# A linear-attention and maxout kernel: eight filling matmuls ahead of a unit's scores become four, between its two score blocks

## The chip, the cores and the metric

The kernel runs on one core of a Trainium2 chip. The metric is the device time in microseconds of one execution. Engines are named as in the profile: PE (TensorE, matmuls; PEld is its weight load), DVE (VectorE), ACT (ScalarE), POOL (GpSimd) and SP (SyncE, which issues most transfers).

## What is computed

Two parts follow each other. The first is a linear attention with a decaying state, for 4 batches, 8 heads, 768 steps and a head size of 48:

```python
for t in range(S):
    cur = np.einsum('bhd,bhe->bhde', u[None] * kt, vt)
    y[:, :, t] = np.einsum('bhd,bhde->bhe', rt, state + cur)
    state = wt[:, :, :, None] * state + np.einsum('bhd,bhe->bhde', kt, vt)
```

The second takes its output as 3072 tokens of 384 numbers through two projections to 1024, takes the larger of the two, and projects back to 384:

```python
h1 = x @ w1
h2 = x @ w2
g = np.maximum(h1, h2)
return (g @ w_out).astype(np.float32)
```

Inputs and output are float32. The kernel uses max(a, b) = relu(a - b) + b: it forms w1 - w2, and folds w2 with w_out into one matrix.

## The kernel before

**Units.** The work is cut into segments of 256 steps. A unit is one segment of one or two batches; there are eight. Units 0 to 3 are the first segment of one batch each, units 4 and 5 the second segment of two batches each, units 6 and 7 the third. Unit 0's work on heads is cut in two halves besides. Within a segment, two neighbouring steps lie on one partition (called j or i, 0 or 1), so 128 partitions hold 256 steps.

**Steps of a unit.** Loads of w, r, k and v; products and logarithms of w; prefix sums by a matmul with a triangle (`ex`, L398); exponentials; r and k scaled by the decays (`scale`, L176 or L180: the tiles rp and kp); their transposes on PE (`tr`, L565) and the copy of these out of PSUM to the tile RK (`te`, L168); the sum of k times v over the segment (`kv`, L596) and its addition to the state (`st`: a copy on ACT and T at L615); the scores of k against r (`sc`, L641); the masked copy of the scores into the tile M (`mk`, L650), whose diagonal has been set from products of r, k and u (`rk` and `ru` for the tile rku, `dg`, `dd`, `di` at L516) and whose other half is zeroed (`zero.M`, L257); the unit's outputs from M and v and from the state (`ya` L688, `yi` L675); then the second part (`gt` L706, `rl` L717, `op` L725 and L729) and its store.

**Scores of unit 0.** `sc.b.j.y` is one block: batch b of the unit, neighbour j, half y of the heads. For unit 0 a block has eight small matmuls. Both blocks of one half share one pair of PSUM banks; a masked copy `mk.b.j.y` takes one block out. The second half's blocks (y = 1) are issued some steps earlier; the blocks sc.0.0.1.0 and sc.0.0.0.0 are the first half's.

**Order.** Every step of every unit stands in one list written out by hand (ORDER, L53 to L114). A loop issues them in that order; each engine takes its own instructions in this order, and waits are set where a step needs another engine's result or a buffer. The letter behind @ names the engine (a for ACT, d for DVE, p for POOL).

**Buffers.** PSUM has four single banks (G), which fills, transposes, prefix sums and turned weights share, and two pairs (Y) for state sums, scores and outputs. A bank that comes free is given to the next step that asks.

**Fills.** `hot.n.x` issues n matmuls of 128x128 by 128x512 on S_b, whose results nobody reads:

```python
def hot(n, _):
    t = bank(F32, "G")
    zz = S_b[:, 0].rearrange("p b q e d -> p (b q e d)")
    for _ in range(n):
        nc.tensor.matmul(t, zz[:, 0:P], zz[:, 0:512], start=True, stop=True)
```

There are six rows of eight in the list, all in its first part (hot.8.0 to hot.8.5). On PE the order around the change is: second transposes of unit 1 (tr.1.0.1), hot.8.1, sc.0.0.1.0, sc.0.0.0.0, hot.8.4, the state sum of unit 1 (kv.1), its other transposes (tr.1.0.0).

## Time and profile before

| | |
|---|---|
| time, median of 3 runs | 146.99 us (146.61 to 147.71) |
| the profiled execution | 147.59 us |
| its span, first to last instruction | 145.9 us |
| busy: PE, DVE, ACT, POOL | 135.3, 116.0, 90.5, 89.3 us |
| fills (L234) | 47 records, 13.3 us busy, mean 435 ns |
| chain that ended last, by engine | PE 42%, DVE 36%, issue 7%, ACT 6% |

Times inside the span count from its start. In a timeline row stand the start, the time that the row took, engine, line, operation, output, inputs, shape and count; idle time ahead of the row and what ended it are in brackets. A row of several matmuls is as long as from the first's start to the last's end; they overlap. One matmul record in some dozens can be missing from a trace.

### The profile page before, as it was taken

The page shows a single profiled execution, that of the slowest core. Times are in us where ns is not written, and L with a number is a line of the kernel's source. Part 1 is how long each engine was busy: PE and PEld are TensorE (multiplying, and loading weights), DVE is VectorE, ACT ScalarE, POOL GpSimd, SP SyncE. Part 2 cuts the span into 40 slices and gives each one's busy share as a digit, 9 for nine tenths or more (in the row PEclk, how much of TensorE's full clock was granted, in tenths as well). Part 3 has the DMA queues.
Part 4 walks back from the last instruction along what each step waited for, and adds up shares of the span by engine and source line. Part 5 has one row for each costly group of instructions (what it writes and reads, how often), then busy time and mean ns, then how long its engine had stood idle before and what let it go on. Part 6 is the DMA issues. An engine that isn't in the chain of part 4 may idle for free.

```text
span 145.9 us, 5536 instructions
## 1 busy us (share of the span) xinstructions
PE 135.3 (93%) x2403; PEld 83.4 (57%) x2404; DVE 116.0 (80%) x162; ACT 90.5 (62%) x164; POOL 89.3 (61%) x106
## 2 busy tenths in 40 slices
PE   5999999789999999999997996999999999999990
PEld 2345654568756757875652563654557545664550
DVE  2489999999999999999998697799966689361411
ACT  4053794997999857999248499378358492227010
POOL 7659979996996389499792917803999900000000
PEclk9999999999999999999999999999999999999999
DMA  3999999999889999986989999699973980061014
GB/s 97 324 324 357 326 415 384 375 311 306 214 220 324 203 264 246 311 220 125 289 130 208 233 309 232 118 137 252 262 250 67 180 214 11 0 216 59 4 62 154
DMA packets 71187, 31.84 MB, mean 218 GB/s; under 512 B 66294, under 2 KB 70391, under 8 KB 71163
## 3 DMA queue, kind: packets, MB, share of 16 engines
q1 hardware_dynamic: 71162, 31.49, 82.9%
q8 instruction: 19, 0.31, 0.9%
q14 instruction: 6, 0.04, 0.1%
HBM read 23.61 MB, written 4.73 MB: 194 GB/s over the span
## 4 chain that ended last, share of the span: by engine, by line
PE 42%; DVE 36%; issue 7%; ACT 6%; POOL 3%; DMA 2%; SPq 2%; DVEq 0%; ACTq 0%
PE G L729 12%; DVE M L650 9%; PE G L706 9%; PE G L234 6%; PE G L725 5%; DVE rp L176 4%; DVE rku L176 3%; DVE dg L502 3%; DVE M L516 3%; DMA RK<-kp 2%; PE Y L688 2%; ACT gT L717 2%; PE Y L641 2%; POOL rku L180 2%; DVE kp L176 2%
## 5 line engine op out<-in xcount | busy, mean ns | idle before, releaser
L729 PE MATMUL G<-wo_sb,gT 128*128 128x384 bf16 x192 | 35.1, 326 | 0.0
L706 PE MATMUL G<-xT,wd_sb 128*128 128x256 bf16 (+1 forms) x192 | 34.2, 326 | 0.6 <-ACT xT L168 0.6
L650 DVE CAST_PREDICATED M<-mask,Y 128x1024 bf16<-128x1024 int32 (+1 forms) x26 | 28.6, 1133 | 4.4 <-PE Y L641 3.6
L717 ACT ACTIVATE gT<-G 128x512 bf16<-128x512 f32 x43 | 24.3, 600 | 10.7 <-PE G L706 10.4
L729 PEld LDWEIGHTS <-gT 128*128 128x128 bf16 x192 | 18.8, 98 | 12.4
L706 PEld LDWEIGHTS <-wd_sb 128*128 128x128 bf16 x192 | 17.9, 98 | 12.4 <-DVE wd_sb L176 0.6
L180 POOL TENSOR_TENSOR kp<-lk,iE 128x384 bf16<-128x384 f32 x16 | 17.1, 1099 | 8.5 <-DVE lk L176 4.2
L725 PE MATMUL G<-wc_sb,xT 128*128 128x384 bf16 x72 | 15.7, 327 | 0.0
L180 POOL TENSOR_TENSOR rku<-rku,u_b 128x384 f32<-128x384 f32 x14 | 14.4, 1052 | 2.0 <-DVE rku L176 2.0
L234 PE MATMUL G<-S_b 128*128 128x512 bf16 x47 | 13.3, 435 | 1.8 <-DVE S_b L263 1.8
L168 ACT COPY RK<-G 128x1024 bf16<-128x1024 bf16 x12 | 12.1, 1017 | 4.7 <-PE G L565 4.7
L168 ACT COPY osb<-G 128x384 f32<-128x384 f32 x7 | 3.3, 478 | 15.2 <-PE G L729 11.9
L180 POOL TENSOR_TENSOR rku<-lr,lk 128x384 f32<-128x384 f32 x8 | 10.5, 1341 | 3.6 <-issue 2.3
L641 PE MATMUL Y<-RK 48*64 48x128 bf16 x384 | 9.0, 220 | 2.6 <-DVE M L650 1.4
L502 DVE TENSOR_REDUCE dg<-rku 128x16 f32<-128x768 f32 x12 | 11.0, 944 | 0.1
L641 PEld LDWEIGHTS <-RK 48*64 48x64 bf16 x384 | 6.1, 106 | 7.8 <-issue 5.9
L168 ACT CAST xT<-Y 128x768 bf16<-128x768 f32 x7 | 7.0, 1027 | 5.7 <-PE Y L675 4.4
L234 PEld LDWEIGHTS <-S_b 128*128 128x128 bf16 x48 | 5.1, 111 | 8.1 <-issue 2.9
L516 DVE TENSOR_TENSOR M<-identq,gd 128x512 int32<-128x512 int32 x12 | 9.2, 778 | 0.4 <-POOL gd L168 0.3
L387 ACT ACTIVATE lg<-lg 128x768 f32<-128x768 f32 (+2 forms) x9 | 5.6, 628 | 6.0 <-DVE lg L176 5.4
L168 ACT CAST S_b<-S_f 64x768 bf16<-64x768 f32 (+1 forms) x14 | 8.7, 623 | 1.0 <-DVE S_f L612 0.8
L176 DVE TENSOR_TENSOR rp<-lr,G 128x768 bf16<-128x768 f32 (+2 forms) x11 | 8.8, 800 | 0.6 <-ACT G L436 0.6
(111 smaller groups left out, 237.5 us busy)
## 6 DMA issues: line engine op xcount, KB each, us to landing
lk<-in_k_dram SPq DMA_DIRECT2D x12, 384.0 KB, 4.9
lv<-in_v_dram SPq DMA_DIRECT2D x12, 384.0 KB, 5.5
lr<-in_r_dram SPq DMA_DIRECT2D x10, 384.0 KB, 5.2
lw<-in_w_dram SPq DMA_DIRECT2D x9, 384.0 KB, 5.1
out_dram<-osb SPq DMA_DIRECT2D x14, 192.0 KB, 4.3
gT<-in_moe_w_dram SPq DMA_DIRECT2D x4, 512.0 KB, 8.4
out_dram<-wb SPq DMA_DIRECT2D x10, 192.0 KB, 2.1
wso<-in_moe_w_out_dram SPq DMA_DIRECT2D x4, 384.0 KB, 5.3
```

The lines of the kernel that those rows point to most:

```text
L168: (nc.scalar.copy if e == "a" else nc.vector.tensor_copy if e == "d" else nc.gpsimd.tensor_copy)(o, i)
L176: op(o, a, b)
L180: op(o[:, g], a[:, g], b[:, g])
L234: nc.tensor.matmul(t, zz[:, 0:P], zz[:, 0:512], start=True, stop=True)
L502: nc.vector.reduce_sum(s.dg[:, b].rearrange("p i h -> p h i"), s.rku[:, b], axis=AX.X)
L516: (nc.vector if en == "d" else nc.gpsimd).tensor_tensor(out=o, in0=m, in1=g.unsqueeze(3).to_broadcast([P, 2, H, Q // 2]), op=ALU.bitwise_and)
L641: nc.tensor.matmul(t[q * Q:(q + 1) * Q, e, p * P:(p + 1) * P].rearrange("s (i g) -> s i g", i=2), s.kT[d, b, j, y * n + p, q, :], s.rT[d, ...
L650: nc.vector.copy_predicated(t[:, :, 2 * n * y:2 * n * (y + 1)].rearrange("s i (p e) g -> s p e i g", e=2), mask[:, j].bitcast(I32).unsquee ...
L706: nc.tensor.matmul(t[:, m * n * P:(m + 1) * n * P].rearrange("c (b t) -> c b t", t=P), wd_sb[:, ko, fo * P:(fo + 1) * P], s.xT[:, 0:n, ko, :],
L717: nc.scalar.activation(o, i, AF.Relu)
L725: nc.tensor.matmul(t[:, 0:HD], s.xT[:, a, ko, :], wc_sb[:, ko, :], start=(ko == 0), stop=False)
L729: nc.tensor.matmul(t[:, 0:HD], s.gT[:, c:c + P], wo_sb[:, f, :], start=False, stop=(f == FO - 1))
```

## The change

The row hot.8.1 is taken out of its place ahead of both blocks of unit 0's first half. A row of four of the same matmuls, hot.4.1, is put in between the two blocks, behind sc.0.0.1.0 and ahead of sc.0.0.0.0. So the program has 44 fills in place of 48. Between the old place and the new stand, for other engines, a load of weights (wload.1.1) and three products of unit 2 (ru.2.0, kw.2.0, scale.2.1.0.0), and for PE the first score block; nothing else changes its order.

```diff
-te.1.0.1@a rk.2.0@d zero.M.2@p di.0.0@d ie.2.0 zero.M.0@p rw.2.0@d hot.8.1 wload.1.1 ru.2.0@d
-kw.2.0@p scale.2.1.0.0@p sc.0.0.1.0 sc.0.0.0.0 mk.0.0.1.0 vb.1.0@a hot.8.4 mk.0.0.0.0 mk.0.0.1.1
+te.1.0.1@a rk.2.0@d zero.M.2@p di.0.0@d ie.2.0 zero.M.0@p rw.2.0@d wload.1.1 ru.2.0@d kw.2.0@p
+scale.2.1.0.0@p sc.0.0.1.0 hot.4.1 sc.0.0.0.0 mk.0.0.1.0 vb.1.0@a hot.8.4 mk.0.0.0.0 mk.0.0.1.1
```

## The prediction

> **What bounds the kernel now.** I read the page first, then the chain of waits around the change, then the engines' timelines there, and last some stretches as windows. The page gives the span and the balance of the engines:

> ```profile
> span 145.9 us, 5536 instructions
> PE 135.3 (93%) x2403; PEld 83.4 (57%) x2404; DVE 116.0 (80%) x162; ACT 90.5 (62%) x164; POOL 89.3 (61%) x106
> ```

> PE is the fullest engine over the whole span, so on this average alone, four matmuls fewer should be a gain. But the average mixes stages. The filling matmuls are at L234, and the ones in question run near 20 us. What ends last there is told by the chain of waits in that stretch (start, us, what), with one undisturbed place further on for comparison:

> ```profile
> 19.97 1.41 DVE rku L176
> 21.38 0.60 DVE M L516
> 21.98 0.47 DVE lr L176
> 22.45 0.10 DVE rku L176
> 22.55 0.49 issue
> ...
> 23.24 1.94 DVE M L650 x4
> ...
> 48.92 0.86 DVE rku L176
> 49.79 0.87 DVE lr L176
> ```

> The chain is on VectorE: product, diagonal (L516), product, product with u, then the four masked copies of unit 0's scores (L650). PE isn't on it. The stretch as a whole, by engine (us from:to, length, then busy time and instructions of each):

> ```profile
> core 0: us, PE busy (x) PEld busy (x) DVE busy (x) ACT busy (x) POOL busy (x), PEclk, DMA share, GB/s
> 16.40:33.00 16.60, 14.27 (x367) 9.89 (x369) 16.59 (x25) 12.98 (x25) 15.39 (x14) 1.00 1.07 366
> ```

> VectorE is busy for 16.59 of 16.60 us: it never waits. That is the bound of the place where the change is made. PE has 2.33 us of holes there, in spite of the fills.

> **The change part by part.** Rows of PE's timeline around the change (start, us, operation, and in brackets the idle time ahead and its releaser):

> ```profile
> 18.26 0.39 PE L565 MATMUL G<-identb,kp 128*128 128x128 bf16 x4
> 18.58 0.42 PE L641 MATMUL Y<-RK 48*64 48x128 bf16 x16
> ...
> 19.97 0.39 PE L565 MATMUL G<-identb,kp 128*128 128x128 bf16 x4
> 20.24 1.89 PE L234 MATMUL G<-S_b 128*128 128x512 bf16 x7
> 22.05 0.42 PE L641 MATMUL Y<-RK 48*64 48x128 bf16 x16
> 22.40 1.90 PE L234 MATMUL G<-S_b 128*128 128x512 bf16 x8
> 24.66 0.44 PE L596 MATMUL Y<-vp,kp 64*64 64x48 bf16 x32 [0.36 <-DVE M L650]
> ```

> The row at 20.24 is the one that goes (one of its eight records is missing: the page counts 47 of 48). The 16 score matmuls at 22.05 are two blocks of eight, sc.0.0.1.0 and sc.0.0.0.0. The new row of four stands between them, so it is behind the first block and still ahead of the second. The row at 22.40 (hot.8.4) stays.

> What one of each kind lasts, by the groups of lines from 25.0 to 28.5 (busy us, mean ns) and by L234's own row (min/median/max ns):

> ```profile
> L565 PE MATMUL G<-identb,rp 128*128 128x128 bf16 x12 | 1.2, 221 | 0.5 <-DVE rp L176 0.5
> L641 PE MATMUL Y<-RK 48*64 48x128 bf16 x16 | 0.4, 222 | 0.0
> ...
> L234 PE MATMUL G<-S_b x47: 376/379/634, 1.8 to 23.9; 128*128 128x512 bf16 x47
> ```

> *PE's own time.* The second row of eight starts its last matmul at 22.40 + 1.90 - 0.38 = 23.92, so one takes 1.52/7 = 0.217 us of issue, and four that go are 0.87 us. Changes from one kind to another cost time too: transposes to scores 0.15 (18.26 + 0.39 - 0.22 = 18.43 to 18.58), fills to scores 0.30 (20.24 + 1.89 - 0.38 = 21.75 to 22.05), scores to fills 0.15 (22.05 + 0.42 - 0.22 = 22.25 to 22.40). The new order in steps: the last transpose starts at 20.14; first score block at 20.29, its last at 20.39; four fills from 20.54, the last at 21.19; second block at 21.49, its last at 21.59, ended by 21.81; hot.8.4 from 21.74, the last at 23.26, ended by 23.64. Before, the scores ended at 22.47 and hot.8.4 at 24.30. So the scores come 0.66 us earlier, and PE is free 0.66 us earlier: 0.87 less some 0.2 for one more change of kind.

> *Can the first block start at 20.29?* It needs the pair of PSUM banks that the sum of unit 0 held and the turned r and k:

> ```profile
> 18.69 1.01 ACT L168 COPY RK<-G 128x1024 bf16<-128x1024 bf16 x1 [0.34 <-PE G L565]
> 19.59 0.59 ACT L168 CAST wb<-G 128x512 bf16<-128x512 f32 x1
> 19.63 0.34 DVE L615 TENSOR_TENSOR T<-Y,S_f 128x192 f32<-128x192 f32 x1
> ```

> The copy ends at 19.70 and T at 19.97; both are done before 20.29. In the old order the fills covered any lateness here; without that cover a late T would hold PE for its lateness, which goes into the hole computed below. The fills' bank was last read by one of the copies above, the latest of which ends at 20.18, before the first fill at 20.54. No other step allocates a bank of that kind between the old and the new place, so the rotation of banks isn't altered. No DMA is issued by the moved steps, and SP's, ACT's, POOL's and VectorE's queues keep their order.

> *Who profits from earlier scores?* Only the masked copies, on VectorE:

> ```profile
> 22.04 0.95 POOL L257 MEMSET M<- 128x1024 bf16 x1 [0.59 <-DVE M L516]
> 22.37 0.94 DVE L176 TENSOR_TENSOR rku<-rku,u_b 128x768 f32<-128x768 f32 x1
> 23.24 1.27 DVE L650 CAST_PREDICATED M<-mask,Y 128x512 bf16<-128x512 int32 x2
> ```

> The product with u runs from 22.37, and the first masked copy starts 0.87 us later; at 48.92, where the next operation is no masked copy, the same step is 0.87 to 49.79. So the copy starts as soon as VectorE is free, though the scores were done at 22.47, and the memset that it also needs at 22.99. The 0.49 of "issue" in the chain is only this product's rest. The gain from the scores is therefore 0, with a bound of 0.02 us by these two rows.

> *Who profits from a free PE?* The next step on PE, the sum of unit 1 (L596) at 24.66, waits for a masked copy, not for the fills: the first two copies end at 23.24 + 1.27 = 24.51, and it starts 0.15 behind. Neither end moves. So its wait grows from 0.36 to 24.66 - 23.64 = 1.02 us, and all behind it in PE's queue (unit 1's other transposes, and the copy on ACT that waited 2.29 us for them) stays where it is:

> ```profile
> 25.69 1.01 ACT L168 COPY RK<-G 128x1024 bf16<-128x1024 bf16 x1 [2.29 <-PE G L565]
> ```

> The sum: 0.87 removed on PE, 0.2 given back, 0.66 into a longer wait, 0 on the path. Below nothing the order has no price either, unless the longer hole changes PE's clock.

> *The clock.* Fills keep PE's clock up; cold matmuls are seen at the start:

> ```profile
> 1.79 5.82 PE L234 MATMUL G<-S_b 128*128 128x512 bf16 x16 [1.79 <-DVE S_b L263]
> ```

> The window row prints a clock of 1.00 even for the first microseconds, so I go by durations: the longest fill took 634 ns against a median of 379, and the first sixteen take 5.82 us, where sixteen at 0.217 would take 3.6. What PE bears without slowing:

> ```profile
> 23.30:26.70 3.40, 2.51 (x51) 1.54 (x49) 3.40 (x7) 1.11 (x2) 3.32 (x4) 1.00 1.03 415
> 26.70:30.10 3.40, 3.12 (x60) 2.56 (x60) 3.40 (x6) 3.28 (x9) 3.40 (x3) 1.00 1.11 341
> 77.00:80.40 3.40, 2.22 (x15) 0.80 (x12) 2.86 (x4) 2.60 (x6) 1.04 (x1) 1.00 1.03 233
> ...
> 80.38 0.42 PE L641 MATMUL Y<-RK 48*64 48x128 bf16 x16 [1.18 <-DMA RK<-kp]
> 90.80 0.42 PE L641 MATMUL Y<-RK 48*64 48x128 bf16 x16 [1.14 <-DVE M L650]
> ```

> The score block at 80.38, behind a hole of 1.18, and that at 90.80, behind 1.14, last the same 0.42 as those at 18.58 and 22.05. The new hole of 1.02 is shorter than either. The stretch from 23.30 falls from 2.51 to about 1.85 busy, below the 2.22 that the clock outlived at 77: a little outside what the trace covers. I take 0, and keep the fall as a rival.

> [...]

> **The rivals.**

> *The clock falls (slower).* Between 25.0 and 28.5 PE does mostly transposes. [...] It decides if the clock falls before 30; PE's 3.12 us from 26.70 to 30.10 would become 6.24 and outrun the stretch by 2.84: about 149.8. For it: the stretch of 1.85. Against: already now a block of scores (222 ns mean, 216 when warm) is all that stands beside transposes, sums and turns of weights from 25.0 to 28.5, and nothing slowed. [...] Chance 0.06.

> *The scores do set the masked copies (faster).* If the hand-over from PE and not the product with u fixed 23.24, everything behind it could come up by as much as the scores, 0.66 us: 146.3. For it: the chain prints "issue" there. Against: the equal 0.87 us in both places. Chance 0.05. This is within 1%.

> *PE's idle time is handed on (faster).* If the sum of unit 1 went with the fills' end after all, it, the transposes and ACT's copy would come 0.66 us earlier; VectorE is full from 16.4 to 33, so at most the same 146.3 comes of it. Against: the wait names VectorE and 24.51 lies behind the fills' 24.30. Chance 0.03.

> *It doesn't do what it says.* Only one block of scores really passes the fills; the other waits for four of them. By the sum that is worth nothing either way, so it is part of the forecast.

> *Something that no row shows*, either way by more than 1%: 0.03 faster, 0.01 slower.

> **How the numbers follow.** The forecast of no change has 0.82. The profiled execution took 147.59 us, 1.69 around its span of 145.9, and 0.60 above the median of the runs, 146.99. Nothing is taken from the path, so span and median stay: 147.0 us. The runs before spread from 146.61 to 147.71; the range takes this spread and reaches down to the two gains of 0.66 (146.3) and a little up: 146.2 to 147.9. That leaves out the clock and the unknown, about 1 in 10. Faster or slower by over 1% (1.47 us) is about what a measurement of this kernel can tell from no change: faster 0.03, within 0.90, slower 0.07.

> **What would show it.** Right: PE has four matmuls fewer and some 0.7 us less busy time; the first scores start near 20.3, the second block near 21.5; the wait of L596 for the masked copies grows from 0.36 to about 1.0; the first masked copy still starts 0.87 behind the product with u, and VectorE stays full from 16.4 to 33. Wrong: a masked copy that starts sooner behind that product; L596 before the second copy's end; or score blocks and transposes between 25 and 33 that last about twice as long, with masked copies waiting for PE.

## The result, and the profile after

The changed kernel takes 148.19 us in the median of 20 runs (146.70 to 150.42), the kernel before 146.96 us (146.38 to 147.81). The ratio is 1.0071, 95% interval 1.0051 to 1.0091: it is slower by 0.7%, about 1.0 us. (The ratio leaves out the two longest runs of the changed kernel, 150.13 and 150.42 us, so it is not the quotient of the two medians, which is 1.008.) The forecast was 147.0 us with a range of 146.2 to 147.9, so the time lies above the range, though within the 1% that the prediction had called no change.

The page of the changed kernel: the span, the engines, and the row of the queue that the page calls instruction.

```profile
span 146.6 us, 5528 instructions
PE 134.1 (91%) x2399; PEld 82.9 (57%) x2400; DVE 116.6 (80%) x162; ACT 90.5 (62%) x164; POOL 90.0 (61%) x106
...
q8 instruction: 19, 0.31, 0.8%
```

PE has 1.2 us less busy time, and the span is 0.7 us longer. (The two profiled executions, 148.34 and 147.59 us, lie closer together than the medians, since that of before was among its longer ones.) At the place of the change nothing of this is to be seen. PE's timeline of the changed kernel there:

```profile
20.31 0.31 PE L641 MATMUL Y<-RK 48*64 48x128 bf16 x8
20.55 1.04 PE L234 MATMUL G<-S_b 128*128 128x512 bf16 x3
21.51 0.31 PE L641 MATMUL Y<-RK 48*64 48x128 bf16 x8
21.75 1.90 PE L234 MATMUL G<-S_b 128*128 128x512 bf16 x8
24.70 0.44 PE L596 MATMUL Y<-vp,kp 64*64 64x48 bf16 x32 [1.05 <-DVE M L650]
25.07 0.40 PE L565 MATMUL G<-identb,rp 128*128 128x128 bf16 x4
...
26.67 0.40 PE L565 MATMUL G<-identb,rp 128*128 128x128 bf16 x4 [0.53 <-DVE rp L176]
```

The score blocks stand at 20.31 and 21.51, PE's wait for the masked copies is 1.05 us, and the sum of unit 1 starts at 24.70, against 24.66 before. The loss comes some seven microseconds later, in the output matmuls of unit 0 (L688). First the kernel before, then the changed one:

```profile
30.30 1.41 PE L688 MATMUL Y<-M,vp 64*32 64x128 bf16 x96
31.64 0.52 PE L675 MATMUL Y<-RK,S_b 128*32 128x128 bf16 x24
32.09 0.43 PE L688 MATMUL Y<-M,vp 64*32 64x128 bf16 x32
33.12 2.13 PE L706 MATMUL G<-xT,wd_sb 128*128 128x256 bf16 x18 [0.60 <-ACT xT L168]
```

```profile
30.33 0.35 PE L688 MATMUL Y<-M,vp 64*32 64x128 bf16 x16
30.83 0.71 PE L688 MATMUL Y<-M,vp 64*32 64x128 bf16 x60 [0.15 <-DVE M L650]
32.73 0.40 PE L688 MATMUL Y<-M,vp 64*32 64x128 bf16 x20 [1.19 <-issue]
33.06 0.52 PE L675 MATMUL Y<-RK,S_b 128*32 128x128 bf16 x24
33.51 0.43 PE L688 MATMUL Y<-M,vp 64*32 64x128 bf16 x32
34.53 2.67 PE L706 MATMUL G<-xT,wd_sb 128*128 128x256 bf16 x23 [0.59 <-ACT xT L168]
```

In the middle of one run of equal matmuls, after 16 + 60 of 96, PE stands still for 1.19 us, and no engine is named: "issue" means that it waited for nothing that the profile shows. From there all is late; L706 starts 1.41 us later than before. The chain of waits of the changed kernel passes through this hole:

```profile
30.83 0.71 PE Y L688 x59
31.54 1.19 issue
32.73 0.40 PE Y L688 x20
```

VectorE gets a hole of its own by it. First its copy of these outputs in the kernel before, which follows the operation ahead of it without a wait, then the same copy in the changed kernel, 1.42 us later:

```profile
32.62 1.02 DVE L168 CAST xT<-Y 128x768 bf16<-128x768 f32 x1
```

```profile
34.04 1.02 DVE L168 CAST xT<-Y 128x768 bf16<-128x768 f32 x1 [1.33 <-PE Y L688]
```

What PE lacked is suggested by this queue, q8, which I take by its name to bring the engines their code: 19 packets with 0.31 MB, so about 16 KB each. Asked for the DMA in narrow stretches, the trace shows the packet next ahead of this place between 28.4 and 28.9 us in the kernel before, and between 30.3 and 30.7 in the changed one:

```profile
q8 instruction: 1, 0.02, 11.4%
```

```profile
q8 instruction: 1, 0.02, 15.5%
```

The last figure is the packet's time as a share of 16 engines: 0.155 x 16 x 0.4 us = 0.99 us (before: 0.114 x 16 x 0.5 = 0.91). So the packet is done by 31.3 to 31.7 us (the packet's own record in the trace: 30.50 to 31.50), and PE goes on at 32.73. That the packet is PE's is so far an inference from the queue's name and the packet's place. An estimate from the trace of the kernel before goes with it: between 28.8 and 137.9 us 17 such packets begin, and PE issues 2128 matmuls with a weight load each, so some 250 instructions to a packet; VectorE, ScalarE and GpSimd issue 309 in that time, 18 to a packet.

### The profile page after: what moved, and what is told of

Same layout as the page of the kernel before. It is cut to its first block, busy times and chain, and to the rows that moved or that the text cites. A ratio compares the mean times of both kernels' runs of the same rounds, so it can differ in the third digit from the quotient of the medians.

```text
span 146.6 us, 5528 instructions
## 1 busy us (share of the span) xinstructions
PE 134.1 (91%) x2399; PEld 82.9 (57%) x2400; DVE 116.6 (80%) x162; ACT 90.5 (62%) x164; POOL 90.0 (61%) x106
## 4 chain that ended last, share of the span: by engine, by line
PE 38%; DVE 34%; issue 7%; DMA 7%; POOL 6%; ACT 4%; SPq 3%; DVEq 0%; POOLq 0%; ACTq 0%
PE G L729 12%; DVE M L650 9%; PE G L706 8%; PE G L725 5%; DVE rp L176 4%; DMA lv<-in_v_dram 4%; DVE rku L176 4%; DVE dg L502 3%; PE Y L688 3%; POOL kp L180 3%; DVE M L516 3%; PE G L234 2%; DMA lw<-in_w_dram 2%; PE Y L675 2%; POOL rku L180 2%
## 5 line engine op out<-in xcount | busy, mean ns | idle before, releaser
L706 PE MATMUL G<-xT,wd_sb 128*128 128x256 bf16 (+1 forms) x192 | 34.2, 326 | 0.6 <-ACT xT L168 0.6
L650 DVE CAST_PREDICATED M<-mask,Y 128x1024 bf16<-128x1024 int32 (+1 forms) x26 | 28.6, 1132 | 2.9 <-PE Y L641 2.0
L706 PEld LDWEIGHTS <-wd_sb 128*128 128x128 bf16 x192 | 17.9, 98 | 12.4 <-issue 0.8
L168 ACT COPY RK<-G 128x1024 bf16<-128x1024 bf16 x12 | 12.1, 1017 | 4.7 <-PE G L565 4.7
L234 PE MATMUL G<-S_b 128*128 128x512 bf16 x43 | 12.0, 429 | 1.8 <-DVE S_b L263 1.8
L180 POOL TENSOR_TENSOR rku<-lr,lk 128x384 f32<-128x384 f32 x8 | 11.6, 1474 | 3.3 <-issue 2.1
L168 ACT COPY osb<-G 128x384 f32<-128x384 f32 x7 | 3.4, 480 | 15.2 <-PE G L729 11.9
L641 PE MATMUL Y<-RK 48*64 48x128 bf16 x384 | 9.2, 221 | 2.4 <-DVE M L650 1.7
L168 ACT CAST xT<-Y 128x768 bf16<-128x768 f32 x7 | 7.0, 1024 | 6.5 <-PE Y L675 5.3
L641 PEld LDWEIGHTS <-RK 48*64 48x64 bf16 x384 | 6.2, 106 | 7.7 <-issue 6.2
L688 PE MATMUL Y<-M,vp 64*32 64x128 bf16 x768 | 9.0, 219 | 1.3 <-issue 1.2
L516 DVE TENSOR_TENSOR M<-identq,gd 128x512 int32<-128x512 int32 x12 | 9.2, 777 | 0.4 <-POOL gd L168 0.3
L176 DVE TENSOR_TENSOR rp<-lr,G 128x768 bf16<-128x768 f32 (+2 forms) x11 | 8.8, 801 | 0.9 <-ACT G L436 0.9
L168 DVE CAST xT<-Y 128x768 bf16<-128x768 f32 x5 | 5.1, 1019 | 5.5 <-PE Y L688 4.5
```

The costliest lines, as they stand in the source:

```text
L168: (nc.scalar.copy if e == "a" else nc.vector.tensor_copy if e == "d" else nc.gpsimd.tensor_copy)(o, i)
L176: op(o, a, b)
L180: op(o[:, g], a[:, g], b[:, g])
L516: (nc.vector if en == "d" else nc.gpsimd).tensor_tensor(out=o, in0=m, in1=g.unsqueeze(3).to_broadcast([P, 2, H, Q // 2]), op=ALU.bitwise_and)
L641: nc.tensor.matmul(t[q * Q:(q + 1) * Q, e, p * P:(p + 1) * P].rearrange("s (i g) -> s i g", i=2), s.kT[d, b, j, y * n + p, q, :], s.rT[d, ...
L650: nc.vector.copy_predicated(t[:, :, 2 * n * y:2 * n * (y + 1)].rearrange("s i (p e) g -> s p e i g", e=2), mask[:, j].bitcast(I32).unsquee ...
```

## The experiments

The theory after this reading, P: PE waited for code. The change takes four matmuls with their weight loads, eight instructions, out of PE's stream, so all later code lies eight places nearer to the program's start, and a block of it, a packet of q8, comes too late. Rivals: the longer hole on PE or its lower activity (H), and the move between the blocks (M). Tiny matmuls (128x8, four of them in 0.24 us) serve to put instructions back without the fills' time: `hot.n.x.m` issues n fills and m tiny ones. The table gives all runs; the text on each follows. In six runs (the changed kernel, e2, e4, e7, e9, e12) PE stops at L688, and in each it goes on 1.2 to 1.5 us after the end of this packet (31.50 and 32.73 in the changed kernel, 31.00 and 32.32 in e7). "Count" is the number of PE instructions against the kernel before; in brackets the part of them that stands behind 25 us.

| run | count | q8 packet begins | wait at L688 | ratio to before (95%) |
|---|---|---|---|---|
| changed kernel | -8 | 30.3 to 30.7 | 1.19 | 1.0071 (1.0051 to 1.0091) |
| e1_pad | 0 | 27.9 to 28.4 | none | 1.0004 (0.9978 to 1.0031) |
| e2_halve | -8 | 29.9 to 30.3 | 0.91 | 1.0074 (1.0046 to 1.0102) |
| e3_move | 0 | 28.4 to 28.9 | none | 1.0003 (0.9978 to 1.0028) |
| e4_padlate | 0 (+8 at 29.8) | 29.9 to 30.3 | 1.19 | 1.0080 (1.0047 to 1.0114) |
| e5_padmid | 0 (+8 at 25.4) | 28.4 to 28.9 | none | 0.9992 (0.9969 to 1.0015) |
| e6_pad2 | -4 | 28.4 to 28.9 | none | 0.9983 (0.9963 to 1.0003) |
| e7_otherrow | -8 | 29.9 to 30.3 | 1.18 | 1.0103 (1.0066 to 1.0140) |
| e8_pad8 | +8 | 28.4 to 28.9 | none | 1.0000 (0.9979 to 1.0021) |
| e9_padbehind | 0 (+8 at 27.3) | 30.3 to 30.7 | 1.15 | 1.0117 (1.0048 to 1.0185) |
| e10_pad1 | -6 | 28.9 to 29.4 | none | 1.0009 (0.9986 to 1.0032) |
| e11_nofill | -4 | 28.4 to 28.9 | none | 1.0019 (0.9980 to 1.0058) |
| e12_loads | -8 | 29.9 to 30.3 | 0.88 | 1.0079 (1.0047 to 1.0111) |
| e13_rpearly | -8 | 29.4 to 29.9 | none named | 1.0017 (0.9990 to 1.0044) |
| e14_rpearly_before | 0 | 28.4 to 28.9 | none | 0.9998 (0.9969 to 1.0028) |
| e15_rpearly_pad2 | -4 | 28.4 to 28.9 | none | 0.9978 (0.9955 to 1.0001) |

**Count, hole or move.**

```diff
 e1_pad, on the changed kernel:   -hot.4.1                      +hot.4.1.4
 e2_halve, on the kernel before:  -hot.8.1                      +hot.4.1  (same place)
 e3_move, on the kernel before:   -hot.8.1 (ahead of both blocks)  +hot.8.1 (between them)
 e4_padlate, on the changed one:  -w2turn.1.1                   +w2turn.1.1.4  (four tiny matmuls first)
```

> The changed kernel plus four tiny matmuls (128x8, with their weight loads: eight instructions) right behind its four fills, so that PE's instruction count ahead of all later code is again that of before, while PE's time for it is nearly that of the changed kernel. Theory P (position in the instruction stream: the code block that PE needs in the middle of unit 0's output matmuls arrives late, because eight instructions fewer stand ahead of it): no wait of about 1.2 us named issue at L688, about 147.0 us. Rival H (the hole of about 1.0 us on PE, or the lower activity behind it, is the cause): the hole is still there, so about 148.2 us, with the wait.

> Only the halving: four fills at the old place, ahead of both score blocks. Theory P: eight instructions fewer, so the late block as in the changed kernel, about 148.2 us with a wait named issue of about 1.2 us at L688. Rival M (the move between the score blocks is the cause): about 147.0 us.

> Only the move: all eight fills between the two score blocks. Theory P: the count is that of before, no late block, about 147.0 us. Rival M: about 148.2 us.

> The changed kernel plus the four tiny matmuls (eight instructions) ahead of the turned weights w2turn.1.1 near 29.8 us, about 250 instructions later than in the first run of this set, ahead of the place where PE waited for code but behind the place where the block before it begins. If it counts where the missing block begins (need): the wait goes or moves by eight instructions, about 147.0 us. If it counts when the block is asked for (trigger: where the block before it begins): the trigger is as in the changed kernel, so the block is as late, about 148.2 us with the wait.

e1 has the changed order with its hole and is as fast as before; e2 has the old order with four fills and is slow; e3 has the new order with eight and isn't. So the move costs nothing, neither does the hole, and the halving costs all of it; e1 shows that it does so by the count. Here stand a row of e1's waits (us in total, times, longest), with the hole still there, and its timeline at L688, which runs through:

```profile
PE Y L596 <- DVE M L650: 1.0, 1, 1.0
```

```profile
31.05 0.91 PE L688 MATMUL Y<-M,vp 64*32 64x128 bf16 x80 [0.15 <-DVE M L650]
```

e4 shows what kind of thing it is. With eight instructions more between the place of the fills and L688, PE stops after 72 of the 96 matmuls and not after 76. Four matmuls with their weight loads are eight instructions:

```profile
30.38 1.08 PE L688 MATMUL Y<-M,vp 64*32 64x128 bf16 x72
32.65 0.45 PE L688 MATMUL Y<-M,vp 64*32 64x128 bf16 x24 [1.19 <-issue]
```

PE stops at a fixed number of instructions from the program's start, whatever these do: the trace counts 346 weight loads ahead of the stop in all six runs with it. I take this for the begin of a block of code. And putting the count right at 29.8 us doesn't bring the block sooner. So the count must matter at an earlier place, which I take for the one where the block is asked for; the trace doesn't show the asking itself.

**Where the asking is held, and how many instructions decide.**

```diff
 e5_padmid, on the changed kernel: -w2turn.2.1   +w2turn.2.1.4   (four tiny matmuls, at 25.4 us)
 e6_pad2, on the changed kernel:   -hot.4.1      +hot.4.1.2
 e7_otherrow, on the kernel before: -hot.8.5     +hot.4.5        (a row near 13 us)
 e8_pad8, on the changed kernel:   -hot.4.1      +hot.4.1.8
```

> The changed kernel plus eight tiny instructions in w2turn.2.1 near 25.5 us: behind PE's wait for the masked copy at 24.6, ahead of its wait for the scaled r (rp) at 26.6. Both theories hold that the block is asked for when PE's reading ahead crosses the block before it. Theory W1 (about 100 instructions ahead, so that the wait at 24.6 holds the asking back when eight instructions are gone): eight more behind that wait don't help, about 148.0 us, with the wait named issue at L688. Theory W2 (about 10 to 17 ahead, so that the wait at 26.6 holds it back): the count ahead of that wait is restored, about 146.8 us and no such wait.

> The changed kernel plus two tiny matmuls (four instructions) behind the four fills: half the count restored. If the asking is held back at one wait, time is all or nothing, either about 146.8 or about 148.0 us. If the cost goes with the count, it is about half, 147.4 us.

> The kernel before with another row of fills halved, hot.8.5 near 13 us; the row ahead of the scores is untouched. Position theory: eight instructions fewer ahead of the same block, about 148.0 us with the wait named issue of about 1 us at L688. If the place of the fills matters, about 146.8 us.

> The changed kernel plus eight tiny matmuls (sixteen instructions) behind the four fills, so eight instructions more than before. Position theory: the block is asked for at least as early as before, about 146.8 us; if the kernel before already lost some time at this or a later block, up to 0.5 us less.

e7 leaves the scores alone, takes four fills out 7 us earlier, and gets the same hole, after the same 76 matmuls:

```profile
32.32 0.40 PE L688 MATMUL Y<-M,vp 64*32 64x128 bf16 x20 [1.18 <-issue]
```

e6 gets all of the time back with half of the count: it is all or nothing. e5 does so with instructions behind the wait at 24.6, so my first thought of a reach of about 100 instructions (W1) fell, and the wait for rp at 26.6 (W2) was left. That PE reads its code ahead, and how far (100 instructions, 10 to 17, sixteen), is theory in these texts and the next, my own estimate; the trace doesn't show the asking. What the runs decide is which of the two waits the late packet goes with.

```diff
 e9_padbehind, on the changed kernel: -tr.2.0.1  +tr.2.0.1.4   (four more transposes of the identity first)
 e10_pad1, on the changed kernel:     -hot.4.1   +hot.4.1.1
 e13_rpearly, on the changed kernel:
-... hot.8.4 mk.0.0.0.0 mk.0.0.1.1 mk.0.0.0.1 vb.1.1@a kv.1 scale.2.0.0.0@d tr.1.0.0
+... hot.8.4 mk.0.0.0.0 scale.2.0.0.0@d mk.0.0.1.1 mk.0.0.0.1 vb.1.1@a kv.1 tr.1.0.0
 e14_rpearly_before: the same move on the kernel before
```

> The changed kernel plus eight instructions (four more transposes of the identity into a bank that is overwritten right after) at the head of tr.2.0.1 near 27.1 us: sixteen instructions behind PE's wait for the scaled r at 26.6, where the eight of e5_padmid stood ahead of it. Theory W2 (the block is asked for when PE's reading, some sixteen instructions beyond the instruction that it is held at, crosses the end of the block before; in the changed kernel it is held at that wait first): they come too late, about 148.0 us with the wait named issue at L688, now after 72 of its 96 matmuls. If any eight instructions ahead of the outputs did: about 146.7 us.

> The changed kernel plus one tiny matmul (two instructions), so six fewer than before. By W2 it is again all or nothing: about 146.7 if the block's end lies within sixteen instructions of the wait, else about 148.0 us. A cost that goes with the count would give 147.5 us or so.

> The changed kernel, with PE's instructions untouched; on VectorE the scaling of r for unit 2 (scale.2.0.0.0) stands two masked copies earlier, so that rp is ready near 25.6 instead of 26.6 us and PE hardly waits for it. Theory W2 (that wait holds back the asking for the code block): with the wait gone the block's transfer starts near 29 us or sooner though eight instructions are missing, the wait named issue at L688 goes, about 146.8 us. Rival C (only the number of instructions ahead matters, the wait at 26.6 has no part in it): transfer near 30.3, the wait at L688 stays, about 148.0 us.

> The kernel before with the same move on VectorE alone. It measures what the move is worth by itself, where the block comes in time: no change, 146.8 us, or up to 0.5 us less, since PE's and ACT's work on unit 2's transposes comes earlier. By either theory no wait at L688.

e9's eight instructions stand sixteen behind the one that waits for rp, and they don't help; e5's stand ahead of it, with one turn of weights (eight instructions) between, and they do. In e9 PE stops after 16 + 56 = 72 matmuls again:

```profile
26.86 0.40 PE L565 MATMUL G<-identb,rp 128*128 128x128 bf16 x4 [0.53 <-DVE rp L176]
...
31.02 0.70 PE L688 MATMUL Y<-M,vp 64*32 64x128 bf16 x56
32.87 0.45 PE L688 MATMUL Y<-M,vp 64*32 64x128 bf16 x24 [1.15 <-issue]
```

The distance can be counted in the changed kernel. From the transposes at 26.67 to the stop PE issues 16 transposes, two score blocks of 16, three turns of four and 76 output matmuls, 136 matmuls, and a weight load with each: 272 instructions, somewhat more than the 250 to a packet of the estimate above. (The trace has one more PE instruction in between, a wait without a matmul at 27.68.) With two more ahead of the wait (e10, 270) the block comes in time, as with four (e6) and eight (e1). So this wait goes with a late block where it stands 272 instructions ahead of the block's begin, and with a timely one where it stands 270 or fewer ahead; greater distances, and other waits, were not tried.

e13 takes the wait away and leaves PE's stream as in the changed kernel, eight short. The transposes follow without one, and the row at L688 has no wait named, but lasts 0.2 us longer than before:

```profile
26.28 0.39 PE L565 MATMUL G<-identb,rp 128*128 128x128 bf16 x4
...
30.65 1.62 PE L688 MATMUL Y<-M,vp 64*32 64x128 bf16 x96
```

The 0.2 us are the rest of the same stop: in a narrow stretch of the trace the last 20 of the 96 matmuls start at 31.87, 0.23 us behind the 76th, and 1.0 to 1.5 us behind the packet's end (0.116 x 16 x 0.5 us = 0.93 us from a begin at 29.4 to 29.9, so 30.3 to 30.8). The packet begins 0.4 to 1.3 us sooner than in the changed kernel, and the ratio falls from 1.0071 to 1.0017. The move alone is worth nothing (e14, 0.9998). By rival C, the bare count, e13 would have stayed at 148.0. It is 147.17: most of the cost went with the wait. By W2 the packet should have begun near 29 us or sooner and the time been 146.8, so W2 is borne out in direction and most of the size, not in all of it.

**The fills, and the transfers.**

```diff
 e11_nofill, on the changed kernel: -hot.4.1  +hot.0.1.6   (no fill, six tiny matmuls)
 e12_loads, on the changed kernel:  woload.3 and woload.2 moved behind load.4.w.0
```

> The changed kernel with no fills in the changed row at all, and six tiny matmuls in their place, so that the instruction count is four fewer than before, as in e6_pad2. If only the position in the stream counts: about 146.6 us, though PE's wait ahead of the sum of unit 1 grows to some 1.8 us. If the fills themselves (PE's activity and clock) are worth something there: slower, 148 us or more, with longer matmuls behind 24.6.

> The changed kernel with two loads of 384 KB each (woload.3 and woload.2) issued behind load.4.w.0 instead of ahead of it; the instructions of PE are the same. If the late block is late because its transfer stands in line behind these loads: its transfer starts earlier than 30.5 us, the wait at L688 shrinks or goes, 146.8 to 147.6 us. If what stands in line doesn't matter: about 148.0 us and a start near 30.4.

e11 can't be told from before by its interval, which reaches to 0.6% slower, but its profile shows what the fills are there for. The hole ahead of L596 is 1.78 us, and behind it matmuls take half as long again. Timeline, then two stretches as windows (PE's clock is the third figure from the end):

```profile
24.61 0.44 PE L596 MATMUL Y<-vp,kp 64*64 64x48 bf16 x32 [1.78 <-DVE M L650]
...
28.40 0.64 PE L641 MATMUL Y<-RK 48*64 48x128 bf16 x16
...
29.93 0.42 PE L641 MATMUL Y<-RK 48*64 48x128 bf16 x16
...
31.30 1.28 PE L688 MATMUL Y<-M,vp 64*32 64x128 bf16 x96
```

```profile
23.00:26.30 3.30, 1.43 (x44) 1.19 (x44) 3.30 (x6) 1.00 (x2) 3.22 (x4) 1.00 1.05 419
27.00:29.60 2.60, 2.60 (x33) 2.23 (x32) 1.99 (x5) 2.19 (x5) 2.60 (x3) 0.50 1.12 352
```

Here the clock did fall to half, for scores at 28.40 that last 0.64 and not 0.42 us. In that execution the outputs of L688 start 1.0 us later than before (31.30 against 30.30), and its time, 147.19 us, lies 0.4 us above the median of before in the same set, 146.76. The other executions have no profile, but five of the ten, this one included, show a mean granted clock of 0.988 or less.

e12 decides nothing. The two loads went back, but the load that came forward is as large (768 KB in all), so the line ahead of the packet wasn't shorter; the packet began at 29.9 to 30.3, and the wait was 0.88 us, which e2 shows (0.91) with the loads in place. Whether the block is slow because of the other transfers is open.

**A version from the cause.**

```diff
 e15_rpearly_pad2, on the changed kernel: -hot.4.1  +hot.4.1.2, and the move of e13
```

> The kernel of e6_pad2 (four fills and two tiny matmuls between the score blocks), the fastest median so far, with the same move on VectorE: a candidate to beat both kernels. 146.2 to 146.8 us, no wait at L688; equal to e14 if the fills' place is worth nothing.

e15 measured 146.51 us, ratio 0.9978 (0.9955 to 1.0001), about that of e6 (146.45 us, 0.9983). Both beat the changed kernel by about 0.9% (0.9978/1.0071 = 0.991, from two sets of runs). Whether they beat the kernel before by 0.2% isn't settled, since both intervals hold 1.

## Why the prediction was wrong

**What held.** Each step at the place of the change came out: the blocks at 20.31 and 21.51 (20.29 and 21.49 forecast), the longer wait at L596 (1.05; 1.02), the start of L596 unmoved, the first masked copy 0.86 us behind the product with u (0.87):

```profile
22.41 0.95 DVE L176 TENSOR_TENSOR rku<-rku,u_b 128x768 f32<-128x768 f32 x1
23.27 2.47 DVE L650 CAST_PREDICATED M<-mask,Y 128x512 bf16<-128x512 int32 x4
```

So the scores are worth nothing to VectorE there, and PE's free time isn't handed on. e3, the move alone, at 1.0003, shows the same in the time. Of the two rivals on the faster side nothing was seen. PE's busy time fell by 1.2 us where some 0.7 was forecast.

**What failed** is the sentence that "all behind it in PE's queue (unit 1's other transposes, and the copy on ACT that waited 2.29 us for them) stays where it is", and with it "0 on the path". It held up to 31.5 us. I had gone through the queues of transfers that SP, ACT, POOL and VectorE feed and left out the one that, by its name, brings PE its code, though q8 is a row of the page. In the sum, the removed instructions stood with their time (0.87 us) alone; their number, eight, had no term. The runs put 1.19 us of waiting in its place, and the median rose by 1.23. That the number and not the time of the instructions is what cost is shown by e1, which puts eight of them back and loses nothing, and by e7, which takes eight out elsewhere and loses as much. The prediction's last rival, "something that no row shows", had 0.01 for slower by over 1% and no mechanism.

**The clock rival** did not come true in the profiled execution: scores and transposes behind 24.70 last as before, and the stretch that was forecast at 1.85 us busy kept its clock:

```profile
23.30:26.70 3.40, 1.82 (x47) 1.23 (x46) 3.40 (x7) 1.10 (x2) 3.32 (x4) 1.00 1.05 417
```

But the clock can fall at this place: e11, with 1.43 of 3.30 us busy, lost the clock where the rival named it. Its price was too high: it put 2.84 us on such a fall, and in e11 the outputs at L688 start 1.0 us later. That PE's time doubles, as this price has it, no row of the kernel before shows; in e11 the granted clock was 0.50, and 16 score matmuls took 0.64 us in place of 0.42. How near the changed kernel came to it there isn't shown. Two of its 20 executions have a lower mean clock (0.985 and 0.989, the others 0.996 or more), and without a profile it is open where they lost it.

**VectorE "stays full from 16.4 to 33"** held to 32.7 and then failed with the block: the wait of 1.33 us for L688 that ends at 34.04, as quoted above, takes up the rest.

## What to carry to other kernels

Here PE runs some 4,800 instructions once, and taking out eight cheap ones ahead of a wait cost 1.19 us of standing still some ten microseconds later. In a kernel like this one look at the queue called instruction in the profile, and at holes named issue inside rows of equal instructions. Where such a hole appears, put the same number of tiny instructions back, far enough ahead of it (here, ahead of the wait that stood 272 instructions before the hole), before judging the edit itself. A change of order and a change of count are best measured apart.

## What the runs showed of the hardware that was not expected

```profile
31.30:34.60 3.30, 1.69 (x127) 1.23 (x104) 1.97 (x3) 1.68 (x5) 3.20 (x4) 1.00 1.12 352
34.70:38.00 3.30, 3.27 (x16) 2.33 (x16) 3.30 (x6) 2.07 (x4) 0.98 (x1) 0.50 0.88 209
```

But neither such a hole nor the busy share of a stretch alone decides: in the same two stretches the clock held at 1.00 in the changed kernel (1.52 of 3.30 us busy in the first, with the hole of 1.19) and in e7 (1.68, with 1.18). What does is open.
- The clock fell more often with the stop at L688. Of the 55 executions of the six kernels with it, 7 show a mean granted clock of 0.989 or less; of the 82 of the eight variants without it that keep at least four fills in the changed row (e1, e3, e5, e6, e8, e10, e14, e15), none; of 107 of the kernel before, run beside them, 2; of ten of e13, which has a rest of the stop, 1. For comparison, the two profiled falls have means of 0.988 (e11) and 0.986 (e9). Where the others fell isn't recorded, so that the stop is the reason isn't shown.
